# Halving the matmul blocks that an ordering list places: two matmuls instead of four

## The chip, the cores and the metric

The kernel runs on one core of one Trainium2 chip, as one program. The metric is the device time of one execution in microseconds (us), the median of three runs.

## The reference

One block of a transformer over 2048 tokens of width 1024, in bf16: a layer norm, attention of 32 heads of width 32 in which a token sees itself and seven earlier ones at steps of two, an output projection with a residual, and then a gated mixer with a second layer norm in the middle and a residual.

```python
def _A_ref(x, wqkv, wo):
    ...
    qkv = (x @ wqkv).reshape(B, S, 3, H, Dh).transpose(2, 0, 3, 1, 4)
    q, k, v = (qkv[0], qkv[1], qkv[2])
    idx = pos[:, None] - off[None, :]          # off = 0, 2, .. 14
    kg = k[:, :, idx_c, :]; vg = v[:, :, idx_c, :]
    logits = einsum('bhsd,bhswd->bhsw', q, kg) * scale
    attn = _softmax(where(idx >= 0, logits, -1e9))
    o = einsum('bhsw,bhswd->bhsd', attn, vg)
    return o.transpose(0, 2, 1, 3).reshape(B, S, D) @ wo

def _B_ref(x, w_in, w_sp, b_sp, w_out):
    z = _gelu(einsum('bsd,df->bsf', x, w_in))  # w_in: 1024 x 3584
    z1 = z[..., :1792]
    z2 = _layernorm(z[..., 1792:])
    g = einsum('ts,bsf->btf', w_sp, z2) + b_sp[None, :, None]   # w_sp: 2048 x 2048
    return einsum('bsf,fd->bsd', z1 * g, w_out)

h = x + _A_ref(_layernorm(x), A_wqkv, A_wo)
h2 = h + _B_ref(_layernorm(h), B_w_in, B_w_sp, B_b_sp, B_w_out)
```

## The kernel before, in words

The tokens go in four chunks of 512 (c = 0 to 3), each of four tiles of 128. The work falls into three parts.

First, up to some 23 us, comes a start written out by hand: warm-up matmuls (L212), the first layer norm, transposes (L283) and the query projection of chunk 0 (L287).

Second, up to 428.5 us, everything that the class `Order` places. Pieces of work are given to it with `add(engine, us, function, deps, prio, take, free)`: an engine, an assumed duration, the code that issues the instructions, what must be done before, a priority (a lower number goes first), and a slot that the piece takes or frees (three PSUM accumulators "acc", one "L", and others). `run` then goes through an assumed clock for each engine, always picks the engine that can start first and on it the ready piece with the lowest priority, and at last issues all pieces in the order of their assumed starts. That order is fixed when the program is built. On the chip each engine runs its own queue strictly in that order and waits at an instruction whose data isn't there.

The pieces of TensorE (PE) in this part are:
- `qkv(c)`: the projections, L439, 16 matmuls for an accumulator of two 128-row blocks (`PIECES` lists block and first of the eight contraction steps). ScalarE (ACT) copies it out (L450) and the copy is stored to DRAM on SyncE's (SP's) DMA queue. Chunk 0's keys and values stay on the chip (L445).
- `attention(c)`: VectorE (DVE) multiplies queries with shifted keys and halves the products (L497 to L507). PE sums them over a head's width into the logits with eight matmuls (L527, called L(c) here). DVE and ACT do the softmax (L536 to L570, exponentials L548). PE spreads the weights of the first four window positions over the partitions with four matmuls (L589, called pb(c)); ACT and DVE copy them out (L594). The other four are spread by a store and loads (L574, L576). DVE then multiplies with the shifted values and adds up (L610 to L621); two of the sums are made by DMAs that GpSimd (POOL) issues (L627). The last L621 of a chunk ends its attention.
- `head(c)`: the output projection, L684, four accumulators of 16 matmuls, called head(c). DVE adds the residual (L693); ACT squares (L698); DVE and POOL make the statistics of the second layer norm (L650 to L657); DVE or ACT normalizes (L727, L730, and L710 for chunk 3); a DMA transposes on SP's queue (L735, L716).
- `b_z2(c)`: the mixer's second half, L761, per tile one accumulator of 1024 columns and one of 768, GELU on ACT (L768), squares on ACT (L777), statistics on DVE (L781 and L650 to L653) and POOL, normalizing on ACT (L791, two halves a tile) or DVE (L793), a store.
- `b_z1(c)`: the mixer's first half, L816, seven accumulators of 16 matmuls a chunk, GELU on ACT (L822), a store.

Projections, z2 and z1 have priorities over 6 in the order in which they are added, the heads 4 and a little, L527 and L589 1. So the long chains of PE are the filler, and attention's and head's pieces cut into them where `run` finds them ready, at the end of a block. Each block's only dependency inside its chain is the block before it. Three accumulators are shared by all of these and by half of each L589.

Third, from 428.5 us, comes the token mixing (L912) and the last projection (L927), in program order.

Of the kernel before, what the change touches and what calls it, by code (L numbers as in the profile page):

```python
# [20 lines left out]
P = 128  # L21
NT = S // P
CH = 512
NCH = S // CH
TPC = CH // P
KT = D // P
DLO = 8
# [9 lines left out]
LSLACK, BSLACK = 2.0, 0.3  # L37
Z2ACT = (4, 4, 4, 0)
L2DVE = (0, 0, 2)
PIECES = ((0, 0), (0, 4), (1, 0), (1, 4))  # L40
LNPRIO = (0, 2.0, 2.5, 2.8)
LAST_COLS = ((0, 512), (512, 896), (896, 1024))

# [84 lines left out]
def kernel(  # L128
# [295 lines left out]
    def order():  # L424
        seq[0] += 1
        return 6.0 + seq[0] * 1e-3

    def qkv(c):
        for xi in range(0 if c else 1, 3):
            wv = wsb[xi][:].rearrange("p kt (m dl) -> p kt dl m", dl=DLO)  # L430
            for dp in range(DLO // 2):
                key = ("acc", "qkv", c, xi, dp)
                deps = [G.get(("xnT", c))]
                for j, k0 in PIECES:
                    def mm(j=j, k0=k0, dl=2 * dp + j, wv=wv, key=key):
                        if j == 0 and k0 == 0:
                            G[key] = new_acc()
                        for kt in range(k0, k0 + 4):
                            T.matmul(G[key][:, j, :].rearrange("p (a b) -> p a b", a=TPC), wv[:, kt, dl, :], xnT[c][:, :, kt, :],  # L439
                                     start=(kt == 0), stop=(kt == KT - 1))  # L440
                    last = add("PE", 0.8634, mm, deps, prio=order(), take="acc" if j == 0 and k0 == 0 else None)
                    deps = [(last, 0.0)]
                def ev(xi=xi, dp=dp, key=key):
                    if c == 0:
                        A.copy(att_in[0][xi][:, 2 * dp:2 * dp + 2, HALO:HALO + CH], G[key][:])  # L445
                        if dp == 3:
                            dma(qkv_d[xi][:, :, CH - HALO:CH], att_in[0][xi][:, :, CH:CH + HALO])
                    else:
                        stg = l1.tile([P, 2, CH], BF16, name="stg", tag="xn", bufs=4)
                        A.copy(stg[:], G[key][:])  # L450
                        dma(qkv_d[xi][:, 2 * dp:2 * dp + 2, c * CH:(c + 1) * CH], stg[:])
                G["ev", c, xi, dp] = add("ACT", 0.92, ev, [last], prio=2.0, free="acc", lat=0.15, take="xn" if c else None)
                if c:
                    dma_op(3.5, lambda: None, [G["ev", c, xi, dp]], free="xn")
            G["wdone", c, xi] = last
        G["qkvlast", c] = last
# [205 lines left out]
    def head(c):  # L662
# [6 lines left out]
        for il in range(TPC):  # L669
            i = c * TPC + il  # L670
            deps = [G["avdone", c]]
            for part in range(4):
                def mm(part=part, il=il, i=i):
                    if part == 0:
                        if il == 0:
                            st["hsum"] = bp.tile([P, TPC], FP32, name="hsum", tag="hsum")
                            st["hsq"] = bp.tile([P, TPC], FP32, name="hsq", tag="hsq")
                            st["hnc"] = bp.tile([P, TPC, D], BF16, name="hb", tag="hb", bufs=1)
                            for k in range(min(XRB, TPC)):
                                xr_load(k)  # L680
                        st["acc", il] = new_acc()
                    for dl in range(2 * part, 2 * part + 2):
                        for nh in range(2):
                            T.matmul(st["acc", il][:, nh, :], oTs[c][:, dl, il * P:(il + 1) * P], wo_sb[:, dl, nh * CH:(nh + 1) * CH],  # L684
                                     start=(dl == 0), stop=(dl == DLO - 1))
                def xr_load(k):
                    st["xr", k] = bp.tile([P, D], BF16, name="xr", tag="xr", bufs=XRB)
                    dma(st["xr", k][:], x2d[(c * TPC + k) * P:(c * TPC + k + 1) * P, :])
                m_ = add("PE", 0.8634, mm, deps, prio=prio + il * 1e-2 + part * 1e-3, take="acc" if part == 0 else None)
                deps = [(m_, 0.0)]  # L690
            def res(il=il, i=i):
                hb = st["hnc"][:, il, :]
                V.scalar_tensor_tensor(hb, st["acc", il][:].rearrange("p a b -> p (a b)"), 1.0, st["xr", il][:],  # L693
                                       op0=ALU.mult, op1=ALU.add, accum_out=st["hsum"][:, il:il + 1])
                dma(h_d[i * P:(i + 1) * P, :], hb)
            r_ = add("DVE", 1.15, res, [m_] + ([G["hdone", c - 1]] if c else []), prio=1.0, free="acc", lat=0.15)
            def hsq(il=il):
                A.activation(st["xr", il][:], st["hnc"][:, il, :], ACTF.Square, accum_out=st["hsq"][:, il:il + 1])  # L698
                if il + XRB < TPC:
                    xr_load(il + XRB)  # L700
            sqd.append(add("ACT", 1.12, hsq, [r_], prio=3.0, lat=0.25))
# [40 lines left out]
    def b_z2(c):  # L742
        st = {}
        sqd = []
        for il in range(TPC):
            evs = []
            for hf in range(2):
                wd = win_specs[hf][1]
                deps = [G.get(("hnT", c, il), G["hnT", c]), G["win", hf]]
                for part in range(4):  # L750
                    def mm(part=part, hf=hf, il=il, wd=wd):
                        if part == 0:
                            st["acc"] = G["accz", c, il, hf] = new_acc()
                            if il == 0 and hf == 0:
                                st["sums"] = bp.tile([P, TPC, 2], FP32, name="sums", tag="sums")
                                st["sqs"] = bp.tile([P, TPC], FP32, name="sqs", tag="sqs")
                        accf = G["accz", c, il, hf][:].rearrange("p a b -> p (a b)")
                        for kt in range(2 * part, 2 * part + 2):
                            for n0 in range(0, wd, CH):
                                n1 = min(n0 + CH, wd)  # L760
                                T.matmul(accf[:, n0:n1], hnTs[c][:, il, kt, :], wins[hf][:, kt, n0:n1],  # L761
                                         start=(kt == 0), stop=(kt == KT - 1))
                    m_ = add("PE", 0.8634 if hf == 0 else 0.650, mm, deps, prio=order(), take="acc" if part == 0 else None)
                    deps = [(m_, 0.0)]
                def ev(hf=hf, il=il, wd=wd):
                    if hf == 0:
                        st["u", il] = l1.tile([P, FH], BF16, name="u", tag="x4k", bufs=4)
                    A.activation(st["u", il][:, hf * 1024:hf * 1024 + wd], G["accz", c, il, hf][:].rearrange("p a b -> p (a b)")[:, 0:wd],  # L768
                                 ACTF.Gelu_apprx_tanh, accum_out=st["sums"][:, il, hf:hf + 1])
                evs.append(add("ACT", 1.02 if hf == 0 else 0.93, ev, [m_] + ([G["z2st", c - 1, il]] if c else []),  # L770
                               prio=2.0, free="acc", lat=0.25, table="gelu"))
            def sq(il=il):
                if c < NCH - 1:
                    junk = pools["bq"].tile([P, FH], BF16, name="junk", tag="junk", bufs=1)[:]
                else:
                    junk = z2sb[c * TPC + il][:]
                A.activation(junk, st["u", il][:], ACTF.Square, accum_out=st["sqs"][:, il:il + 1])  # L777
            sqd.append(add("ACT", 1.72, sq, evs + ([G["close"]] if c == NCH - 1 else [G["open"]]), prio=5.0, lat=0.25))
# [27 lines left out]
    def b_z1(c):  # L806
        for fp in range(NF // 2):
            deps = [G["hnT", c], G["win", 2 if fp < 4 else 3]]
            for j, k0 in PIECES:
                def mm(j=j, k0=k0, fp=fp):  # L810
                    f = 2 * fp + j
                    wt, f0 = (wins[2], f) if f < 8 else (wins[3], f - 8)
                    if j == 0 and k0 == 0:
                        G["accy", c, fp] = new_acc()
                    for kt in range(k0, k0 + 4):
                        T.matmul(G["accy", c, fp][:, j, :].rearrange("p (a b) -> p a b", a=TPC), wt[:, kt, f0 * P:(f0 + 1) * P],  # L816
                                 hnTs[c][:, :, kt, :], start=(kt == 0), stop=(kt == KT - 1))
                m_ = add("PE", 0.8634, mm, deps, prio=order(), take="acc" if j == 0 and k0 == 0 else None)
                deps = [(m_, 0.0)]
            def ev(fp=fp):  # L820
                z1s = l1.tile([P, 2, CH], BF16, name="z1s", tag="xn", bufs=4)
# [151 lines left out]
```

## Time and profile before

| what | value |
|---|---|
| median of three runs | 724.37 us (724.16 to 726.34) |
| the profiled execution | 723.34 us, span of its instructions 721.6 us |
| granted TensorE clock | 1.000 of full speed |
| PE busy | 714.1 us, 99% of the span |
| DVE, ACT, POOL busy | 420.8, 217.7, 51.2 us |
| DMA | 113.12 MB, 157 GB/s on the mean |

The engines run side by side, so the busy times overlap. Matmuls are pipelined: a matmul's own duration (379 ns for 512 columns) is longer than the distance from one start to the next. In a row of the timeline stand the start in us, the duration, the engine, the source line, the operation, the tiles written and read, their shapes and a count; in square brackets, the idle time of the engine just before, and what ended it. In a row of the waits stand who waited for whom, the sum in us, how often, and the longest.

### The profile page before, as it was taken

The numbers are of one execution on the slowest core, as the hardware profiler recorded it, in microseconds if no ns is written. First come the engines' busy times: TensorE is split into PE (matmuls) and PEld (weight loads), VectorE is DVE, ScalarE is ACT, GpSimd is POOL, SyncE is SP. The second block draws the span as 40 slices with busy tenths as digits, with TensorE's granted clock in tenths as the row PEclk, the third lists the DMA queues.
The fourth block names the chain that finished last, engine by engine and source line by source line (L and its number), as shares of the span: only waits on it lengthen the run. The fifth ranks groups of instructions, "written<-read, shape, count | busy, mean of one in ns | idle before, by whom it ended". The sixth has DMA issues, their size and how long they took to land.

```text
span 721.6 us, 8559 instructions
## 1 busy us (share of the span) xinstructions
PE 714.1 (99%) x3493; PEld 370.3 (51%) x3537; DVE 420.8 (58%) x470; ACT 217.7 (30%) x280; POOL 51.2 (7%) x61
## 2 busy tenths in 40 slices
PE   8999999999999999999999999999999999999998
PEld 7766665666545444445445444444444444444444
DVE  6899899999999799988951103222222222222222
ACT  4523432533348866738825420000000000000000
POOL 0100010012110111000204100000000000000000
PEclk9999999999999999999999999999999999999999
DMA  9964697389973594642849899163016411120002
GB/s 327 322 185 110 201 215 206 128 233 277 312 301 58 188 238 142 233 117 66 223 129 294 230 299 295 48 148 116 29 45 128 132 33 45 35 86 11 0 17 71
DMA packets 117590, 113.12 MB, mean 157 GB/s; under 512 B 68080, under 2 KB 95120, under 8 KB 117424
## 3 DMA queue, kind: packets, MB, share of 16 engines
q1 hardware_dynamic: 108528, 75.48, 35.7%
q0 software_dynamic: 8448, 36.64, 17.6%
q8 instruction: 27, 0.44, 0.3%
q10 hardware_dynamic: 576, 0.47, 0.2%
q14 instruction: 11, 0.09, 0.0%
HBM read 57.19 MB, written 31.26 MB: 123 GB/s over the span
## 4 chain that ended last, share of the span: by engine, by line
PE 98%; DMA 0%; DVE 0%; issue 0%; ACT 0%
PE acc L912 27%; PE acc L439 21%; PE acc L816 13%; PE acc L761 13%; PE acc L927 13%; PE acc L684 8%; PE acc L287 2%; DMA xp<-in_A_x_dram 0%; PE L L527 0%; PE tpt L283 0%; PE pb L589 0%; DVE bnst L242 0%; DVE xn L272 0%; DVE bnst L243 0%; PE tpa L283 0%
## 5 line engine op out<-in xcount | busy, mean ns | idle before, releaser
L912 PE MATMUL acc<-wspT,z2sb 128*128 128x512 bf16 x878 | 193.1, 379 | 0.9
L912 PEld LDWEIGHTS <-z2sb 128*128 128x128 bf16 x896 | 87.7, 98 | 105.7
L915 DVE TENSOR_TENSOR g<-acc,bB 128x1024 bf16<-128x1024 f32 x28 | 34.3, 1224 | 160.2 <-PE acc L912 127.9
L816 PE MATMUL acc<-hnT,win 128*128 128x512 bf16 x448 | 98.0, 379 | 0.0
L761 PE MATMUL acc<-win,hnT 128*128 128x512 bf16 (+1 forms) x501 | 97.4, 352 | 0.6
L761 PEld LDWEIGHTS <-hnT 128*128 128x128 bf16 x512 | 49.9, 98 | 47.5 <-issue 0.7
L497 DVE TENSOR_TENSOR prod<-qT,kT 128x4096 bf16<-128x4096 bf16 x32 | 72.4, 2283 | 0.0
L927 PEld LDWEIGHTS <-zg 128*128 128x128 bf16 x462 | 44.7, 98 | 52.4
L816 PEld LDWEIGHTS <-win 128*128 128x128 bf16 x448 | 43.7, 98 | 52.6 <-issue 0.7
L450 ACT CAST stg<-acc 128x1024 bf16<-128x1024 f32 x36 | 36.4, 1011 | 77.2 <-PE acc L439 66.4
L934 DVE TENSOR_TENSOR ot<-acc,hr 128x1024 bf16<-128x1024 f32 x15 | 18.4, 1225 | 69.4 <-PE acc L927 60.5
L927 PE MATMUL acc<-wout_a,zg 128*128 128x512 bf16 (+2 forms) x260 | 58.0, 373 | 0.3
L439 PE MATMUL acc<-xnT,wk 128*128 128x512 bf16 x256 | 56.5, 380 | 0.0
L439 PE MATMUL acc<-xnT,wv 128*128 128x512 bf16 x256 | 56.1, 380 | 0.0
L684 PE MATMUL acc<-wo_sb,av_oT 128*128 128x512 bf16 x250 | 55.6, 379 | 0.3
L439 PEld LDWEIGHTS <-wv 128*128 128x128 bf16 x256 | 36.7, 144 | 18.5 <-issue 0.2
L439 PEld LDWEIGHTS <-wk 128*128 128x128 bf16 x256 | 36.6, 144 | 18.7 <-issue 0.7
L927 PE MATMUL acc<-wout_b,zg 128*128 128x512 bf16 (+2 forms) x193 | 43.8, 373 | 0.2
L439 PE MATMUL acc<-xnT,wq 128*128 128x512 bf16 x192 | 42.1, 380 | 0.0
L684 PEld LDWEIGHTS <-av_oT 128*128 128x128 bf16 x256 | 25.0, 98 | 30.1
L822 ACT ACTIVATE z1s<-acc 128x1024 bf16<-128x1024 f32 x28 | 28.6, 1022 | 37.8 <-PE acc L816 33.5
L501 DVE TENSOR_TENSOR prod<-prod 128x2048 bf16<-128x2048 bf16 x32 | 38.4, 1217 | 0.1
(140 smaller groups left out, 562.1 us busy)
## 6 DMA issues: line engine op xcount, KB each, us to landing
qkv_d<-stg SPq DMA_DIRECT2D x36, 256.0 KB, 3.9
z_d<-z1s SPq DMA_DIRECT2D x28, 256.0 KB, 2.6
z1c<-z_d SPq DMA_DIRECT2D x28, 256.0 KB, 2.8
z_d<-u SPq DMA_DIRECT2D x12, 448.0 KB, 2.8
z2sb<-z_d POOLq DMA_DIRECT2D x12, 448.0 KB, 9.7
xr<-in_A_x_dram SPq DMA_DIRECT2D x16, 256.0 KB, 3.1
av_y<-av_z POOLq DMA_DIRECT2D x4, 1024.0 KB, 8.6
av_oT<-av_zz POOLq DMA_DIRECT2D x4, 1024.0 KB, 12.1
```

The source lines that it names most:

```text
L439: T.matmul(G[key][:, j, :].rearrange("p (a b) -> p a b", a=TPC), wv[:, kt, dl, :], xnT[c][:, :, kt, :], start=(kt == 0), stop=(kt == KT - 1))
L450: A.copy(stg[:], G[key][:])
L497: V.tensor_tensor(st["prod"][:], qT[:], kT[:, :, o:o + CH], op=ALU.mult)
L501: V.tensor_tensor(dst, p_[:, 0:4, :], p_[:, 4:8, :], op=ALU.add)
L684: T.matmul(st["acc", il][:, nh, :], oTs[c][:, dl, il * P:(il + 1) * P], wo_sb[:, dl, nh * CH:(nh + 1) * CH], start=(dl == 0), stop=(dl == ...
L761: T.matmul(accf[:, n0:n1], hnTs[c][:, il, kt, :], wins[hf][:, kt, n0:n1], start=(kt == 0), stop=(kt == KT - 1))
L816: T.matmul(G["accy", c, fp][:, j, :].rearrange("p (a b) -> p a b", a=TPC), wt[:, kt, f0 * P:(f0 + 1) * P], hnTs[c][:, :, kt, :], start=(kt ...
L822: A.activation(z1s[:], G["accy", c, fp][:], ACTF.Gelu_apprx_tanh)
L912: T.matmul(acc[:, j, :], z2sb[a][:, f * P:(f + 1) * P], wspT[:, a, :], start=(a == 0), stop=(a == NT - 1))
L915: V.tensor_tensor(g1[:], acc[:], bB[:, c * CH:(c + 1) * CH].unsqueeze(1).to_broadcast([P, 2, CH]), op=ALU.add)
L927: T.matmul(outs, zg[:, f, il * P:(il + 1) * P], wt[:, f0, lo:hi], start=(f == 0), stop=(f == NF - 1))
L934: V.tensor_tensor(ot[:], acc[:].rearrange("p a b -> p (a b)"), hr[:], op=ALU.add)
```

## The change

In projections, heads, z2 and z1 the pieces given to `Order` hold two matmuls instead of four, and twice as many pieces are given, each with half the assumed duration (0.4317 instead of 0.8634 us; 0.325 instead of 0.650 in z2's narrower half). Matmuls, their order within a chain and the accumulators are the same. The order of everything in the second part is planned anew from these pieces.

```diff
-PIECES = ((0, 0), (0, 4), (1, 0), (1, 4))
+PIECES = tuple((j, k0) for j in range(2) for k0 in range(0, 8, 2))
...
 # qkv(c)
-                        for kt in range(k0, k0 + 4):
+                        for kt in range(k0, k0 + 2):
                             T.matmul(G[key][:, j, :].rearrange("p (a b) -> p a b", a=TPC), wv[:, kt, dl, :], xnT[c][:, :, kt, :],
                                      start=(kt == 0), stop=(kt == KT - 1))
-                    last = add("PE", 0.8634, mm, deps, prio=order(), take="acc" if j == 0 and k0 == 0 else None)
+                    last = add("PE", 0.4317, mm, deps, prio=order(), take="acc" if j == 0 and k0 == 0 else None)
...
 # head(c)
-            for part in range(4):
+            for part in range(8):
...
-                    for dl in range(2 * part, 2 * part + 2):
-                        for nh in range(2):
-                            T.matmul(st["acc", il][:, nh, :], oTs[c][:, dl, il * P:(il + 1) * P], wo_sb[:, dl, nh * CH:(nh + 1) * CH],
-                                     start=(dl == 0), stop=(dl == DLO - 1))
+                    for nh in range(2):
+                        T.matmul(st["acc", il][:, nh, :], oTs[c][:, part, il * P:(il + 1) * P], wo_sb[:, part, nh * CH:(nh + 1) * CH],
+                                 start=(part == 0), stop=(part == DLO - 1))
...
-                m_ = add("PE", 0.8634, mm, deps, prio=prio + il * 1e-2 + part * 1e-3, take="acc" if part == 0 else None)
+                m_ = add("PE", 0.4317, mm, deps, prio=prio + il * 1e-2 + part * 1e-3, take="acc" if part == 0 else None)
...
 # b_z2(c)
-                for part in range(4):
+                for part in range(8):
...
-                        for kt in range(2 * part, 2 * part + 2):
-                            for n0 in range(0, wd, CH):
-                                n1 = min(n0 + CH, wd)
-                                T.matmul(accf[:, n0:n1], hnTs[c][:, il, kt, :], wins[hf][:, kt, n0:n1],
-                                         start=(kt == 0), stop=(kt == KT - 1))
-                    m_ = add("PE", 0.8634 if hf == 0 else 0.650, mm, deps, prio=order(), take="acc" if part == 0 else None)
+                        for n0 in range(0, wd, CH):
+                            n1 = min(n0 + CH, wd)
+                            T.matmul(accf[:, n0:n1], hnTs[c][:, il, part, :], wins[hf][:, part, n0:n1],
+                                     start=(part == 0), stop=(part == KT - 1))
+                    m_ = add("PE", 0.4317 if hf == 0 else 0.325, mm, deps, prio=order(), take="acc" if part == 0 else None)
...
 # b_z1(c): as qkv(c), with its own operands
```

More of the change, by code (lines that the diff above doesn't have):

```diff
@@ L814, in mm @@
                         G["accy", c, fp] = new_acc()
-                    for kt in range(k0, k0 + 4):
+                    for kt in range(k0, k0 + 2):
                         T.matmul(G["accy", c, fp][:, j, :].rearrange("p (a b) -> p a b", a=TPC), wt[:, kt, f0 * P:(f0 + 1) * P],
                                  hnTs[c][:, :, kt, :], start=(kt == 0), stop=(kt == KT - 1))
-                m_ = add("PE", 0.8634, mm, deps, prio=order(), take="acc" if j == 0 and k0 == 0 else None)
+                m_ = add("PE", 0.4317, mm, deps, prio=order(), take="acc" if j == 0 and k0 == 0 else None)
                 deps = [(m_, 0.0)]
```

## The prediction

> **What bounds the kernel now.** I read the page first (busy shares, then the chain that ended last), then the waits of TensorE, then the stretches by window, then the timeline around each place where the change moves something.
>
> ```profile
> PE 714.1 (99%) x3493; PEld 370.3 (51%) x3537; DVE 420.8 (58%) x470; ACT 217.7 (30%) x280; POOL 51.2 (7%) x61
> ...
> PE 98%; DMA 0%; DVE 0%; issue 0%; ACT 0%
> ```
>
> TensorE (PE) is busy in 99% of the span and is 98% of the chain. The waits of PE, all of them:
>
> ```profile
> PE wps L212 <- DVE eps_t L213: 1.2, 1, 1.2
> PE tpt L283 <- DVE xn L272: 1.0, 1, 1.0
> ```
>
> Both lie in the first 7 us, which the change doesn't touch. From 23.2 us, where the planned order begins, PE waits for nothing. What can still be won there follows from the spacing. Twelve matmuls of 512 columns start in 2.58 us (362.69 to 365.27), so one takes 0.215. Around the first gather of weights of chunk 1 (L589), four matmuls from 163.07 should end at 163.93 and L589 starts at 164.03; its last starts at 164.04 and the next matmul at 164.36, 0.32 later. A short insertion thus loses about 0.2 us. There are eight (four L527, four L589), 1.6 us together, and the changed program has as many. **No order of the same matmuls can win over 1.6 us, 0.22%.** A measurement of this kernel can tell about 0.3% (2.2 us) from no change, so the question is whether PE now has to wait.
>
> **What moves on PE.** The instruction order of the changed program has the same matmuls; all blocks of one chain still follow each other, except where L527 (logits), L589 (weights spread) or the output heads L684 cut in. Those now cut in at a boundary of two matmuls, and earlier: of the twelve places, L(0) and head(0) stay, L(1), pb(0), pb(1), head(1), L(2), head(2) come 2 matmuls earlier, pb(2), L(3), pb(3) 4, and head(3) 6. That is 0.43, 0.86 and 1.29 us at 0.215; in z2's narrower half, where 12 matmuls take 1.96 us (194.63 to 196.59), a pair is 0.33, so head(1) moves by 0.33 and L(3) by 0.65. Each place waits for DVE, and the whole PE queue stands behind it. So I compare each move with the time between the end of the DVE instruction needed and PE's start. The tightest two, and then a loose one:
>
> ```profile
> 194.01 2.29 DVE L621 TENSOR_TENSOR av_oT<-av_oT,av_b 128x4096 bf16<-128x4096 bf16 x1
> ...
> 196.59 0.59 PE L684 MATMUL acc<-wo_sb,av_oT 128*128 128x512 bf16 x2
> ```
>
> ```profile
> 246.17 1.29 DVE L570 TENSOR_TENSOR attn<-sme,rinv 128x512 bf16<-128x512 f32 x2
> ...
> 247.22 0.39 PE L589 MATMUL pb<-attn,csb 32*128 32x512 bf16 x2
> ```
>
> ```profile
> 361.48 2.29 DVE L621 TENSOR_TENSOR av_oT<-av_oT,av_b 128x4096 bf16<-128x4096 bf16 x1
> ...
> 365.27 5.99 PE L684 MATMUL acc<-wo_sb,av_oT 128*128 128x512 bf16 x26
> ```
>
> Slack against move: head(1) 196.59 - 196.30 = 0.29 against 0.33; pb(2), whose first half of the weights ends 0.69 after 246.17, 0.36 against 0.86; head(3) 1.50 against 1.29; pb(0) 1.31 against 0.43; L(1) 0.52 against 0.43; pb(1) 0.77 against 0.43; L(2) 0.49 against 0.43; head(2) 0.62 against 0.43; L(3) 1.44 against 0.65; pb(3) 1.36 against 0.86. Were DVE's times to stay, only pb(2) would wait, 0.50, and head(1) 0.04; a wait, once had, delays PE at all later places, so these don't add and the bill is 0.50.
>
> **What DVE and ACT gain or lose.** DVE doesn't stay: it waits for the very instructions that come earlier. It stood idle 1.59, 1.18, 1.17 and 2.11 us for L527 and 1.18, 0.64, 0.23 and 1.23 for L589. So the attention chain moves forward with PE's order, chunk by chunk:
> - Chunk 0: DVE is up to 0.43 earlier at head(0). After it, the second residual L693 waited 1.08 for the head; two products' additions now stand before it instead of one (1.22), which fills that wait. L(1) then has some 1 us of slack.
> - Chunk 1: L(1) and pb(1) pass 0.43 on, so head(1) has 0.29 + 0.43 - 0.33 = 0.39; if the spread's store and loads eat the gain (L613 waited 0.80 for them), it is 0.29 - 0.33, a wait of 0.04. I take 0.
> - Chunk 2, before L(2): the statistics of l2 stand behind one more product (2.28), so the transposed chunk for z2(1) comes some 2 us later. It was in time by far: the transpose issues at 224.16 for 4.88, z2(1) starts at 254.6. On ACT its two normalizing instructions (1.23 each) now delay the squares of z2(0) by about 1 us: their end goes from 232.2 to about 233.4. DVE's five small instructions that need them (L781 to L653, at 233.75 now) would arrive at 233.3, 0.43 earlier than now. They wait 0.1 to 0.2, and L(2), 3.7 us behind them, is ready at 237.2 for a PE that comes at 237.50. I take 0, with 0.3 as the upper end.
> - Chunk 2, after L(2): now an eviction (L822) and two table loads stand around the exponentials, and DVE waits for that:
>
> ```profile
> 240.42 1.02 ACT L822 ACTIVATE z1s<-acc 128x1024 bf16<-128x1024 f32 x1 [1.04 <-PE acc L816]
> 241.46 1.28 ACT L548 ACT_TABLE_LOAD   x1
> 242.75 1.15 ACT L548 ACTIVATE sme<-sme 128x512 f32<-128x512 f32 x2
> 243.42 0.94 DVE L552 TENSOR_TENSOR ssum<-sme 128x256 f32<-128x256 f32 x2 [2.27 <-ACT sme L548]
> ```
>
> In the changed order a third half of L791 (1.12, in place of one after) stands there and the eviction comes behind the exponentials. ACT is free at 240.4, loads until 241.7, and the first half of the weights is ready 1.0 earlier, at 245.8; pb(2) comes at 247.22 - 0.86 = 246.36. The 0.50 above vanishes. The price is that eviction: it ends at 242.9 + 1.28 + 1.02 = 245.2 instead of 241.4, and the next user of its accumulator (one of three) is the second half of pb(2) at 246.4. Covered by 1.2 us.
> - Head(2): the first residual now stands before the statistics of z2(1), so its normalizing on ACT starts 3 us later, and its stores with it. Their buffers are rewritten one by one by z2(2), from 320.3 on, each over 20 us after its store. SP's transpose for head(2) goes ahead of two z1 stores, which wait out its 4.84 us; their four buffers turn over in 4 x 16 matmuls, 13.8 us. The same for head(0)'s transpose and one projection store. Nothing.
> - Chunk 3: the copy of the spread weights (L594) now stands on ACT before a square of 1.69 us, not behind it, so DVE's products start 1.0 earlier and head(3) has 1.50 + 1.0 - 1.29 = 1.2 us.
> - After head(3) ten matmuls of z1 are left instead of four, and z2(3) begins at the same place. The mixing stage (from 428.5) is unchanged.
>
> **The sum.** Gain on PE 0, bounded by 1.6; loss 0 to 0.5, taken as 0.1. The profiled execution took 723.34 us at a span of 721.6 and would take 723.4. The median of the three runs is 724.37, 1.03 over it, so I put the changed kernel at 724.4.
>
> **The rivals.** Slower, by a queue that blocks: DVE's five small instructions before L(2) wait for ACT's squares, and PE's L(2) for DVE. This decides once the squares end later than 233.7, 0.3 over my sum; every further microsecond is one on PE. ACT had 0.65 and 2.43 us of idle just behind, so the delay can't come from its load, only from its order; two more instructions of 1.2 ahead of the squares than I count would cost 2.1 us and give 726.5; three, 727.7. For it: the two tightest sums meet here. Against: I count only one 1.1 us displacement. Chance 0.09 that it costs over 2.2.
>
> Slower, by the stores: at 192.68 ACT stood 3.70 us because a projection's store hadn't landed.
>
> ```profile
> 192.68 1.01 ACT L450 CAST stg<-acc 128x1024 bf16<-128x1024 f32 x1 [3.70 <-DMA qkv_d<-stg]
> ```
>
> That accumulator is next needed by head(1), 2.9 us after the copy, and 2.6 in the new order. Another meeting of stores, weight loads and gathers must delay the landing by 4.8 us to cost 2.2: 726.6. The order of these queues is the same and shifts by 0.4. Chance 0.05.
>
> Slower, by the clock. PE changes between groups no oftener than now, and the page's row of the granted clock has 9s throughout; after 0.99 us of idle at 6.31 the transposes run at full rate. The eleven slow matmuls at the start (L212) took 4.13 us instead of 11 x 0.215 = 2.37: at most 1.8 us for each time the clock fell. Two falls give 728. Chance 0.01. The Trainium skill, page TensorE: Matmul & The Clock Gate, section A second HAM failure mode, holds that short idle times between groups of matmuls can make the clock swing to half rate, which speaks against finer cuts. By that rule each swing would cost this kernel as above; the trace disagrees, as its insertions leave the clock full.
>
> Nothing happens at all, since only the order of 30 matmuls around insertions changes: that is my forecast.
>
> **Chances.** Within 0.3%: 0.82. Slower 0.15 (0.09, 0.05, and the clock's 0.01). Faster 0.03: only by a measurement off by more than the 1.6 us that order can win. The range starts at 724.4 - 1.6 = 722.8 and reaches into the first rival, to 727.0.
>
> **What would show it.** After: PE's waits still only the two of the first 7 us; L527's idle on DVE smaller by the moves; in chunk 2 L552 waiting about 1 us less; L684 of head(3) at 363.98; mixing from 428.5. A wait of PE at L527 near 237.5 or at L684 near 196.3 would show the rivals; PE idle of over 2.2 us anywhere behind 23 us makes the prediction wrong.

## The result, and the profile after

The changed kernel takes 730.13 us (median of 22 runs, 723.11 to 736.54); the kernel before took 723.89 us in the same comparison (22 runs, 723.19 to 726.34). The ratio is 1.006 [1.0044, 1.0075]: slower, by more than 0.3%. (The ratio is near that of the means of the fast executions, without the changed kernel's three slowest, 734.68 to 736.54 us, and so are the ratios below; the medians here differ by 0.9%.) The forecast was 724.4 us, 722.8 to 727.0. The times of the changed kernel spread over 13 us, those of the kernel before over 3. Four of the 22 took under 724 us with the same order of matmuls, so the loss is had in most executions and not in all.

The profiled execution took 731.43 us at a span of 729.6; before it was 721.6. The page's busy row and chain (line numbers after the change are one or two lower than before: L910 is before's L912, L913 its L915):

```profile
PE 717.4 (98%) x3493; PEld 371.0 (51%) x3537; DVE 421.0 (58%) x470; ACT 217.6 (30%) x280; POOL 52.1 (7%) x61
...
PE 96%; DMA 2%; DVE 1%; issue 0%; SPq 0%; ACT 0%
```

PE fell from 98% of the chain to 96%, and DMA came in with 2%. The waits of PE, all of them:

```profile
PE acc L910 <- DVE g L913: 5.3, 1, 5.3
PE wps L212 <- DVE eps_t L213: 1.2, 1, 1.2
PE acc L910 <- issue: 0.2, 1, 0.2
```

One wait is new, and it isn't in the part that the change touches. L910 is the mixing matmul, L913 the addition of the bias that frees its accumulator. The same place by windows (before the wait and in it, the 5 us behind it, the 4 us behind those; PEclk is the granted clock):

```profile
core 0: us, PE busy (x) PEld busy (x) DVE busy (x) ACT busy (x) POOL busy (x), PEclk, DMA share, GB/s
446.00:454.40 8.40, 3.28 (x16) 1.37 (x14) 1.08 (x1) 0.00 (x0) 0.00 (x0) 0.91 0.62 190
454.60:459.70 5.10, 4.88 (x12) 1.79 (x13) 4.32 (x5) 0.00 (x0) 0.00 (x0) 0.50 1.08 368
459.80:464.00 4.20, 4.20 (x21) 1.87 (x20) 0.00 (x0) 0.00 (x0) 0.00 (x0) 1.00 0.48 152
```

PE stood from 449.28 to 454.60. Behind that it had half the clock: 12 matmuls in 5.1 us, where 12 at 0.215 take 2.6. So 5.3 + 0.2 + 2.5 = 8.0 us, and the spans differ by 729.6 - 721.6 = 8.0. Nothing is left to explain on PE.

**Why the bias comes late.** The first g of the two kernels (DVE's timeline, before and then after):

```profile
443.59 1.23 DVE L915 TENSOR_TENSOR g<-acc,bB 128x1024 bf16<-128x1024 f32 x1 [32.23 <-DMA z1c<-z_d]
```

```profile
453.32 1.22 DVE L913 TENSOR_TENSOR g<-acc,bB 128x1024 bf16<-128x1024 f32 x1 [41.90 <-DMA z1c<-z_d]
```

PE fills three accumulators, 96 matmuls from 428.4, and needs the first one back at about 449.2. Before, g had freed it at 444.8, 4.4 us ahead; after, at 454.5. The row names the z1c load as the last to come, but what g needs is the bias bB, whose load lands at 443.27 before and 453.00 after. SP issues it, and SP was held up (SP's timeline, before and then after):

```profile
418.17 15.56 SPq L834 DMA_TRANSPOSE wspT<-in_B_w_sp_dram  x1
433.82 2.19 SPq L823 DMA_DIRECT2D z_d<-z1s  x4
438.74 0.34 SPq L901 DMA_DIRECT2D bB<-in_B_b_sp_dram  x1
```

```profile
418.81 23.61 SPq L832 DMA_TRANSPOSE wspT<-in_B_w_sp_dram  x1
442.51 2.77 SPq L821 DMA_DIRECT2D z_d<-z1s  x4
448.60 0.34 SPq L899 DMA_DIRECT2D bB<-in_B_b_sp_dram  x1
```

The second transpose of the mixing weights (called wspT1 below) begins 0.6 us later and holds SP 8 us longer; four z1 stores and the bias stand behind it. It runs against POOL's two loads of wout (the weights of the last projection), which land at 424.5 and 428.9 before and at 438.0 and 442.3 after. These wait for the first such transpose (wspT0; it lands at 412.87 before, 419.36 after), which waits for the last z2 load (402.60; 408.33). And the z2 loads start right behind head(3), where they meet head(3)'s fourth transpose. SP's timeline there, before and then after:

```profile
381.25 0.37 SPq L823 DMA_DIRECT2D z_d<-z1s  x1
381.71 3.39 SPq L716 DMA_TRANSPOSE hnT<-hb  x2
```

```profile
379.77 1.29 SPq L715 DMA_TRANSPOSE hnT<-hb  x1
381.45 0.38 SPq L821 DMA_DIRECT2D z_d<-z1s  x1
382.19 1.27 SPq L715 DMA_TRANSPOSE hnT<-hb  x1
```

And the DMA issues around the fourth transpose, before (383.8 to 384.0) and after (381.4 to 382.3, where the last z1 store of chunk 2 is issued too); the last figure is the time from issue to landing:

```profile
z2sb<-z_d POOLq DMA_DIRECT2D x1, 448.0 KB, 4.0
hnT<-hb SPq DMA_TRANSPOSE x1, 6.1
```

```profile
z2sb<-z_d POOLq DMA_DIRECT2D x1, 448.0 KB, 4.3
z_d<-z1s SPq DMA_DIRECT2D x1, 256.0 KB, 2.4
hnT<-hb SPq DMA_TRANSPOSE x1, 14.5
```

The transpose took 14.5 us instead of 6.1, and the loads beside it were slow as well: after, the DMA engines were full from 386 to 397 at 192 GB/s, and moved 282 GB/s at a share of 0.73 once the transpose was through.

```profile
386.00:397.00 11.00, 10.95 (x58) 5.62 (x58) 0.00 (x0) 7.61 (x12) 0.90 (x3) 1.00 1.05 192
397.00:408.00 11.00, 11.00 (x59) 5.59 (x57) 0.82 (x5) 6.62 (x11) 1.94 (x4) 1.00 0.73 282
```

So the theory, **A**: the change moves head(3) ahead of six more matmuls of z1. Its transposes and POOL's z2 loads then meet in a way that drags both out (first meeting); the end of the z2 loads passes the delay on to wspT0 and to wout; wout's loads then lie on wspT1 for longer (second meeting); SP issues the bias 10 us late, and PE has 4.4 us of margin. The rivals: **B**, the finer blocks themselves cost (spacing, clock, evictions); **C**, the place of the last z1 store of chunk 2 on SP, which now stands between the third and the fourth transpose; **D**, that store's 256 KB being in flight when the fourth transpose starts.

### The profile page after: what moved, and what is told of

It reads as the page before. It is cut to its first block, busy times and chain, and to the rows that moved or that the text cites. A ratio compares the mean times of both kernels' runs of the same rounds, so it can differ in the third digit from the quotient of the medians.

```text
span 729.6 us, 8557 instructions
## 1 busy us (share of the span) xinstructions
PE 717.4 (98%) x3493; PEld 371.0 (51%) x3537; DVE 421.0 (58%) x470; ACT 217.6 (30%) x280; POOL 52.1 (7%) x61
## 4 chain that ended last, share of the span: by engine, by line
PE 96%; DMA 2%; DVE 1%; issue 0%; SPq 0%; ACT 0%
PE acc L910 26%; PE acc L439 21%; PE acc L814 13%; PE acc L759 13%; PE acc L925 13%; PE acc L683 8%; PE acc L287 2%; DMA z1c<-z_d 1%; DMA z_d<-z1s 1%; DMA xp<-in_A_x_dram 0%; PE L L527 0%; PE tpt L283 0%; SPq L821 0%; DVE xn L272 0%; DVE bnst L242 0%
## 5 line engine op out<-in xcount | busy, mean ns | idle before, releaser
L910 PE MATMUL acc<-wspT,z2sb 128*128 128x512 bf16 x878 | 195.6, 382 | 6.4 <-DVE g L913 5.3
L910 PEld LDWEIGHTS <-z2sb 128*128 128x128 bf16 x896 | 88.2, 98 | 113.1 <-issue 8.9
L913 DVE TENSOR_TENSOR g<-acc,bB 128x1024 bf16<-128x1024 f32 x28 | 34.3, 1223 | 168.3 <-PE acc L910 126.4
L759 PE MATMUL acc<-win,hnT 128*128 128x512 bf16 (+1 forms) x501 | 97.4, 352 | 0.6
L759 PEld LDWEIGHTS <-hnT 128*128 128x128 bf16 x512 | 49.9, 98 | 47.6 <-issue 0.7
L766 ACT ACTIVATE u<-acc 128x1024 bf16<-128x1024 f32 (+1 forms) x32 | 29.3, 915 | 33.0 <-PE acc L759 33.0
```

The source lines that it names most:

```text
L759: T.matmul(accf[:, n0:n1], hnTs[c][:, il, part, :], wins[hf][:, part, n0:n1], start=(part == 0), stop=(part == KT - 1))
L910: T.matmul(acc[:, j, :], z2sb[a][:, f * P:(f + 1) * P], wspT[:, a, :], start=(a == 0), stop=(a == NT - 1))
L913: V.tensor_tensor(g1[:], acc[:], bB[:, c * CH:(c + 1) * CH].unsqueeze(1).to_broadcast([P, 2, CH]), op=ALU.add)
```

## The experiments

The median of the kernel before is 723.33, 723.54 and 723.39 us in the three groups that follow (e1 to e4, e5 to e8, e9 to e12). The ratios are to the kernel before in the same group.

**The kernel after, once more** (e1; no edit).

> The changed kernel as it is, profiled a second time. Theory A (two meetings of transposes with POOL's loads): the loss is one wait of PE in the mixing stage of 0 to 8 us, ended by DVE's first L913, plus a stretch at half clock of 2 to 3 us where the wait is long; it goes with the time at which the fourth transpose of head(3) lands, and no other row of PE differs from before. Times between 723 and 737. Theory B (the new order on PE itself loses time): the loss is spread over the second part, before 428.5, and is the same in each execution.

730.1 us, ratio 1.0075 [1.0049, 1.0101]; PE waits 3.4 us, first g at 451.83. The loss repeats; its size varies with the execution. One row that I had not expected is new: z2(3) waits 0.2 us (L759) for the fourth transpose, which lands at 398.55 here.

**The first meeting taken away** (e2): the z2 loads wait for the fourth transpose.

```
-  nc.sync.dma_start_transpose(hnTs[c][:, il], ...)
+  G["tr3"] = nc.sync.dma_start_transpose(hnTs[c][:, il], ...)
...
   zl.append(dma_w(z2sb[i][:], z2_d[i * P:(i + 1) * P, :]))
+  if i == 0: tc.add_manual_dep(zl[0].ins, G["tr3"].ins.name, wait_for, ...)
```

> The changed kernel with the first z2 load on POOL made to wait until the fourth transpose of head(3) has landed. Theory A: the transpose lands within 3 us of its issue, near 385; the twelve loads then take 12 x 1.13 us and land near 400; the first transposed mixing weights issue near 402 to 403 and the output weights' loads near 413, as before the change; PE waits 0 to 1 us in the mixing stage; 723.4 to 725. Rival C (only the second meeting, of output weights and the second transposed mixing weights, matters, and it comes about by itself): unchanged, 728 to 732. Theory B: unchanged.

723.29 us, ratio 1.0003 [0.9994, 1.0012]. The DMA issues at 382.5 to 382.7, and DVE's first g:

```profile
hnT<-hb SPq DMA_TRANSPOSE x1, 3.1
```

```profile
445.62 1.23 DVE L915 TENSOR_TENSOR g<-acc,bB 128x1024 bf16<-128x1024 f32 x1 [33.79 <-DMA z1c<-z_d]
```

Alone, the transpose takes 3.1 us. The loads, begun 4.6 us later, end at 404.41 (I had expected them near 400), 4 us earlier than after, and the rest follows: no wait of PE in the mixing stage. With the same matmul order as after, the loss is gone, so B falls.

**The second meeting taken away** (e3): wout's loads are issued behind wspT1 and wait for it, not for wspT0.

```
-  tc.add_manual_dep(i_.ins, wsp_ins[0].ins.name, wait_for, ...)
...
-  load_wsp(c + 1)
+  w_ = load_wsp(c + 1)
+  if c == 0:   # the two loads of wout
+      tc.add_manual_dep(i_.ins, w_.ins.name, wait_for, ...)
```

> The changed kernel with the loads of the output weights made to wait for the second transposed mixing weights instead of the first. Theories A and C alike: the transpose takes some 15.6 us on SP's queue instead of 23.6 and ends near 434, DVE's first L913 comes near 444 and PE doesn't wait; 723.4 to 725 whatever the first meeting does (the output weights land near 450, before PE needs them at 476). Theory B: unchanged, 728 to 732.

723.27 us, ratio 0.9998 [0.999, 1.0007]. SP's and DVE's timelines:

```profile
418.48 8.66 SPq L832 DMA_TRANSPOSE wspT<-in_B_w_sp_dram  x1
```

```profile
441.24 1.23 DVE L911 TENSOR_TENSOR g<-acc,bB 128x1024 bf16<-128x1024 f32 x1 [29.96 <-DMA bB<-in_B_b_sp_dram]
```

The first meeting is still there (the fourth transpose lands at 397.27, the z2 loads at 408.92), but wspT1 holds SP for 8.7 us instead of 23.6. Both meetings are needed for the loss.

**The last link** (e4, then e8): the bias is loaded on ACT's queue into memory of its own, ahead of everything on SP.

```
-  bB = p2.tile([P, S], BF16, name="bB", bufs=1)
+  bB = pools["bB"]   # a tile of its own
-  dma(bB[:], B_b_sp.unsqueeze(0).to_broadcast([P, S]))
+  i_ = A.dma_start(bB[:], B_b_sp.unsqueeze(0).to_broadcast([P, S]))
+  tc.add_manual_dep(i_.ins, G["gelu"].ins.name, wait_for, ...)   # the last GELU
```

> The changed kernel with the bias (bB) loaded from ACT's DMA queue behind the last GELU instead of from SP's, where it stands behind the blocked transpose. If the bias is what DVE's first L913 waits for: that instruction starts at 436 to 440, two accumulators are free before PE needs them at 449.2, PE waits 0, 723.4 to 725, though both meetings still take place. If the z1 loads hold DVE as well (L914 behind the first L913 on the same queue): PE waits up to 2 us less than in the plain changed kernel or nothing changes, 726 to 731.

724.55 us, ratio 1.0023 [1.0005, 1.004]. In the profiled execution (727.22 us) PE still waits 2.1 us, and the expectation of the first g was missed:

```profile
449.97 1.22 DVE L915 TENSOR_TENSOR g<-acc,bB 128x1024 bf16<-128x1024 f32 x1 [38.71 <-DMA z_d<-z1s]
```

The bias had landed at 438.38, but g waited for the last z1 store (landed 449.65): g's tile lies in the memory of z1's staging buffers, and that store is behind wspT1 on SP as well. To tell whether this was all, the next kernel gives g's tile a place of its own too (`g1 = pools["z"].tile(..., bufs=2)`):

> As the run with the bias on ACT's queue, and the tile g that L913 writes also lies in memory of its own, not where the z1 buffers were, whose last store lands behind the blocked transpose. If that reuse is what held L913 at 449.97: L913 starts when the bias lands, 437 to 441, PE waits 0 though both meetings take place and the second mixing weights take over 20 us; 723.3 to 724.5. If something else holds it: a wait of 2 us stays, 724 to 728.

```profile
437.49 1.23 DVE L916 TENSOR_TENSOR g<-acc,bB 128x1024 bf16<-128x1024 f32 x1 [25.42 <-DMA bB<-in_B_b_sp_dram]
```

723.77 us, ratio 1.0007 [0.9999, 1.0016], no wait of PE in the mixing stage. Here both meetings are as bad as after (fourth transpose 382.35 to 398.75, wspT1 23.2 us on SP), and the mixing stage doesn't notice. So they cost next to nothing by themselves; what costs is the bias and g's buffer behind them. What this run still shows of the first meeting is a short wait of PE in z2(3) for the fourth transpose:

```profile
PE acc L759 <- DMA hnT<-hb: 0.3, 1, 0.3
```

**Which part of the change does it** (e5, e6). First head(3)'s move alone, in the kernel before: only the last z1 accumulator of chunk 2 goes in twos, and its last five blocks wait for head(3), which so cuts in with ten matmuls left.

```
+  fine = c == 2 and fp == NF // 2 - 1
-  for j, k0 in PIECES:
+  for j, k0 in PIECES2 if fine else PIECES:
...
+  G["hold"].deps.append((G["headmm", NCH - 1], 0.0))
```

> The kernel before, with one thing of the change alone: head(3) cuts into the last z1 accumulator of chunk 2 after 6 matmuls instead of 12, so that 10 are left behind it and the store of that accumulator stands between the third and the fourth transpose of head(3). Theory A with the store as its trigger: the fourth transpose lands 12 to 16 us after its issue, the first mixing weights issue near 408, the output weights' loads come behind the second mixing weights, PE waits 2 to 6 us in the mixing stage; 728 to 732. Rival D (it takes other parts of the new order): as before, 723.2 to 724.

730.33 us, ratio 1.0072 [1.0042, 1.0101]. DMA issues around 382, and PE's wait:

```profile
z2sb<-z_d POOLq DMA_DIRECT2D x1, 448.0 KB, 4.6
hnT<-hb SPq DMA_TRANSPOSE x1, 15.4
```

```profile
PE acc L917 <- DVE g L920: 6.1, 1, 6.1
```

One move of twelve brings the whole loss. Then the rest of the change without it: the kernel after, with z1 alone back in blocks of four (head(3) then stands where it did before).

> The changed kernel with z1 alone in blocks of four again; projections, heads and z2 stay in twos. head(3) then cuts in after 12 matmuls and the store stands before the third transpose, as before the change. Theory A with the store as its trigger: the fourth transpose lands within 8 us, PE waits 0 to 1 us; 723.3 to 724.5. Rival D (the finer blocks elsewhere): 728 to 732.

723.5 us, ratio 1.0003 [0.9994, 1.0011]; the transpose takes 6.3 us, wspT1 15.3 us on SP, and PE waits nowhere in the mixing stage. The finer blocks of projections, heads and z2 cost nothing and win nothing.

**C** (e7): the kernel after with that store issued on ACT's queue instead of SP's (`A.dma_start` for `c == 2`, last `fp`).

> The changed kernel, the store of chunk 2's last z1 accumulator issued on ACT's DMA queue, so that it isn't in front of the fourth transpose on SP's; its time stays. If its place in SP's queue is what hurts: the fourth transpose lands within 8 us of its issue, 723.3 to 725. If its packets on the engines hurt, on whichever queue, or if what hurts is that z2 loads meet the transpose at all: unchanged, 728 to 732.

732.51 us (4 runs), ratio 1.0121 [1.0106, 1.0136]: no better. The fourth transpose is issued at 382.09 with no store in front of it on SP, and takes 15.5 us, no less than the 14.5 of after:

```profile
hnT<-hb SPq DMA_TRANSPOSE x1, 15.5
```

C falls. The store is still in flight there (381.31 to 383.67), on ACT's queue.

**D** (e9, e10): the first kernel was to issue the store behind the fourth transpose.

> The kernel after, with the last z1 store of chunk 2 issued behind head(3)'s fourth transpose in place of before it. The fourth transpose (about 382.2) and the first z2 load (about 381.9) should begin as in the kernel after; only the store's 256 KB are no longer on the DMA engines when the two begin. Theory 'the store in flight makes the transpose late': the fourth transpose lands by about 390 as in the kernel before, the z2 loads end by about 403, no wait of PE in the mixing stage, 723.5 us. Theory 'the z2 loads alone do it, by starting within a few tenths of the transpose while the transposes are under way': it lands at 396 to 399 as in the kernel after, wspT1 lands at 440 or later, PE waits 3 to 7 us in the mixing stage, 727 to 732 us.

Its edit did not move the store on SP: it is issued at 381.45, the transpose at 382.18, as in the kernel after. So it tells nothing of the store and repeats the kernel after: 730.43 us, ratio 1.0075 [1.0052, 1.0098], PE waits 4.1 us. The other kernel leaves the store alone and holds the first z2 load until it has landed:

```
   zl.append(dma_w(z2sb[i][:], z2_d[i * P:(i + 1) * P, :]))
+  if i == 0: tc.add_manual_dep(zl[0].ins, G["store", NCH - 2, NF // 2 - 1].ins.name, wait_for, ...)
```

> The kernel after, with the first z2 load waiting for the landing of the last z1 store of chunk 2 (383.7 in the kernel after), so that POOL's loads start near 384, some 1.8 us behind the fourth transpose instead of 0.25 us ahead of it. Theory 'the store in flight makes the transpose late': nothing changes for the transpose, it lands at 396 or later, PE waits 3 to 7 us, 727 to 732 us. Theory 'what counts is which of the two is on the engines first': the transpose is through its reads for the most part when the loads come, lands by about 388, the z2 loads end near 403, no wait of PE, 723.4 us.

723.52 us, ratio 1.0001 [0.9992, 1.0011]. The store is in flight from 381.96 to 384.34, over the first half of the fourth transpose, issued at 382.69, and that takes

```profile
hnT<-hb SPq DMA_TRANSPOSE x1, 3.1
```

The z2 loads came at 385.37, 1.4 us later than I had expected, and their first packet starts at 386.7, so that they didn't meet the transpose at all (it lands at 385.74). With the store beside it and without the loads it is as quick as in e2, where the store was in flight too (381.86 to 384.24). So the store alone doesn't drag it out, and D falls as far as that. Without the loads nothing is dragged out; whether the store adds to what the loads do isn't tested, since every run of the new order that has the loads there has the store there too.

**Can it be better?** (e11, e12) The kernel after with both remedies, and the kernel before with wout behind wspT1:

> The kernel after with both remedies: the first z2 load waits for head(3)'s fourth transpose, and the two wout loads wait for wspT1. Each alone took the wait away; if the finer order is worth what the sum of the prediction left it (at most 1.6 us) it shows here, where nothing else is late: 722 to 723 us. If PE's own work sets the time, it is 723.3 us, as with either alone, and first g stands near 441 or earlier.

> The kernel before with the two wout loads waiting for wspT1 (order of matmuls unchanged). Theory 'two meetings of a transpose with large-packet loads hold the first g back': wspT1 takes about 9 us of SP's time instead of 15.6, lands before 430, and the first g moves from 443.6 to 441 or earlier. PE did not wait there, so the median stays at 723.3 us (722.9 to 723.8); what it could change is the upper end of the times, if the 725 to 726 us runs of the kernel before come from the same meeting.

723.66 us, ratio 0.9997 [0.9987, 1.0008], and 723.47 us, ratio 1.0007 [0.9996, 1.0017]. Neither beats the kernel before: PE's work sets the time. Both missed the expectation of the first g, which came at 444.61 and 445.33, not near 441, though wspT1 shrank to 7.5 and 7.6 us on SP. The wout loads now begin at 428.8 and 428.6, and the last z1 store, issued 1.2 to 1.3 us behind them, takes 9.1 and 9.2 us to land (2.4 in e3, where it went 0.3 us ahead of them); the bias waits for it. So this remedy can trade one meeting for another. Nor did the upper end of the times change in e12 (726.11).

## Why the prediction was wrong, step by step

**Right: PE's own order.** All twelve places stand 0.05 or 0.06 us behind the forecast, which is the shift that the first of them (L527 at 75.02 for 74.96), not moved by the change, already has. The three that were shown, in PE's and DVE's timeline after:

```profile
192.97 2.29 DVE L621 TENSOR_TENSOR av_oT<-av_oT,av_b 128x4096 bf16<-128x4096 bf16 x1
...
196.32 1.03 PE L683 MATMUL acc<-wo_sb,av_oT 128*128 128x512 bf16 x4
...
245.19 1.29 DVE L570 TENSOR_TENSOR attn<-sme,rinv 128x512 bf16<-128x512 f32 x2
246.42 0.39 PE L589 MATMUL pb<-attn,csb 32*128 32x512 bf16 x2
...
360.33 2.29 DVE L621 TENSOR_TENSOR av_oT<-av_oT,av_b 128x4096 bf16<-128x4096 bf16 x1
...
364.04 2.32 PE L683 MATMUL acc<-wo_sb,av_oT 128*128 128x512 bf16 x9
```

Forecast: 196.26, 246.36, 363.98. DVE did come earlier with PE (head(1)'s slack is 196.32 - 195.26 = 1.06, not the 0.39 I had), and no place of the second part waits for DVE. How thin head(1)'s 0.29 was in the order of before, e12 shows, which has that order: PE waited 0.2 us for DVE's L621 there. The 0 to 0.5 us of loss there measured 0, and the gain bounded by 1.6 measured 0 too (e6, e11).

**Right: chunk 2 behind L(2).** The eviction went behind the exponentials and the softmax came 1.0 us earlier (L552 at 242.44 for 243.42). Its wait shrank by only 0.6, from 2.27 to 1.66, since DVE itself got there 0.4 sooner:

```profile
240.48 1.28 ACT L548 ACT_TABLE_LOAD   x1
241.78 1.15 ACT L548 ACTIVATE sme<-sme 128x512 f32<-128x512 f32 x2
242.44 0.94 DVE L552 TENSOR_TENSOR ssum<-sme 128x256 f32<-128x256 f32 x2 [1.66 <-ACT sme L548]
```

**Wrong: "After head(3) ten matmuls of z1 are left instead of four, and z2(3) begins at the same place. The mixing stage (from 428.5) is unchanged."** PE's side of it holds: the mixing starts at 428.39. But I followed the queues behind head(0) and head(2) and not behind head(3), where the move is largest and where, besides SP's transposes, POOL's z2 loads start. That the two get in each other's way the trace of before did show: head(3)'s second and third transposes landed 3.1 and 3.2 us after their issue, the fourth, with the loads beside it, 6.1. I gave it no price. The term was 0 and measured 8.0 us in the profiled execution, 6 to 7 in the medians.

**Missed: the margin at 449.2.** The trace of before has the row (DVE's waits):

```profile
DVE g L915 <- DMA z1c<-z_d: 32.2, 1, 32.2
```

The first g of the mixing waits for DMA, and PE comes back for its accumulator 4.4 us after it ends. PE waits for nothing there, so no row of PE's waits shows it. "PE waits for nothing" is a statement on one order; the margin was the number to have.

**The rivals.** None was this one. L(2) on DVE's five small instructions: not seen, PE's L527 starts at 237.56 without a wait. The stores: the copy at 191.48 now waits for PE, not for a store:

```profile
191.48 1.01 ACT L450 CAST stg<-acc 128x1024 bf16<-128x1024 f32 x1 [2.44 <-PE acc L439]
```

The clock: it did fall, once, at a price of 2.5 us instead of at most 1.8; but behind a long wait, not between short cuts, so its cause in the rival was wrong. No 0.3 us insertion moved it here either.

**What stays open.** The first z2 load is 0.2 us ahead of the fourth transpose in the kernel before and in e6, and 0.25 ahead in the kernel after; the transpose takes 6.1 to 6.3 us there and 14.5 here. In both the third transpose is on its way when the first load is issued and has landed when that load's first packet starts (384.9 and 385.0 before, 382.8 and 383.5 after), so that isn't the difference. Before, the fourth's 1024 packets go through in one burst, most of them between 387 and 388; after, some 450 go between 385 and 386 and the rest trickle until 396. What on the DMA engines decides between burst and trickle isn't settled. That the loads must be there is. The store isn't ruled out as a part of it. In the kernels with 6.1 to 6.3 us (before, e6, e12) it had landed before the fourth transpose and the first z2 load were issued (383.57 against 383.87 and 383.68 in the kernel before); in all eight with 14.5 to 16.4 us (after, e1, e3, e4, e5, e7, e8, e9) it landed some 1.5 us behind the transpose's issue. Against it speaks that after, its last packet starts at 383.4, ahead of the first packet of the loads and of the fourth transpose (384.5).

## What to carry to other kernels

A change of order on the bound engine also moves the DMA triggers behind it: of every moved step list what each queue issues next, and which transfers then share the engines for the first time or in another order. Where the bound engine waits for nothing, work out the margin of each handover to it anyway; here 4.4 us of margin at one accumulator decided, 70 us behind the cause. Transposes by DMA are best kept apart from large loads by a dependency rather than by luck of timing: at this place that wait (e2) cost nothing measurable.

## What the runs showed of the hardware

- **A DMA transpose and POOL's loads drag each other out.** Head(3)'s fourth transpose (packets of 256 bytes) took 3.1 us alone, 6.1 to 6.3 us beside z2 loads (packets of 7 KB), and 14.5 to 16.4 us beside them where head(3) cuts in earlier (why is open); wspT1 held SP 7.5 to 8.7 us alone and 15 to 25 beside wout. While mixed, in the kernel after, single packets of the loads, usually 0.28 us, took up to 5.9 us. The Trainium skill, page DMA: Bandwidth & Descriptors, section SWDGE vs HWDGE vs iDMA, has each DMA engine take turns, packet by packet, between the queue that POOL feeds and the one that SP feeds. An estimate by it, if each packet in the trace is one turn, which no run here shows: the transpose has 1024 packets, 64 for each of 16 engines, each behind one of 0.28 us, 18 us in all. That is near the 14.5 us measured after and the 15.4 in e5, but it explains neither the 6.1 us of before, nor the 450 packets that go in one us after, nor the packets of 5.9 us.
- **The clock falls behind a single wait, and a shorter one than expected.** In the profiled execution after, the granted clock was 1.00 for the first 3.6 us of the 5.3 us wait and 0.50 from then (452.9) to 459.7, so that PE's first 5.1 us of work ran at half rate. In e7 it fell 2.2 us into a wait of 7.3, in e5 4.7 us into one of 6.1. The Trainium skill, page TensorE: Matmul & The Clock Gate, Part 1, has half rate after an idle window of some 3.4 us, and full rate again after as long a busy one; here PE worked for 5.1 us until the rate was full again, and in e4 the clock was at 0.50 for 3.4 us (451.74 to 455.15), so the trace agrees roughly with the second figure. But in e4 PE waited only 2.1 us and still had half the clock soon after:

```profile
449.10:451.20 2.10, 0.02 (x1) 0.00 (x0) 1.22 (x1) 0.00 (x0) 0.00 (x0) 1.00 0.13 20
451.30:453.00 1.70, 1.70 (x5) 0.65 (x6) 0.40 (x1) 0.00 (x0) 0.00 (x0) 0.63 1.00 296
453.00:455.00 2.00, 1.78 (x5) 0.65 (x5) 1.97 (x3) 0.00 (x0) 0.00 (x0) 0.50 0.90 289
```

The measurement decides: here a wait of 2.1 us was enough, and its price was 725.4 - 721.6 = 3.8 us of span, not 2.1.
